# A delta-rule attention kernel: one product of K with [Q | state] in four 64x64 places, with a new order of program blocks

## The chip, the cores and the metric

The kernel runs on one core of a Trainium2 chip. The metric is the device time of one execution in microseconds (us). A kernel is timed in several runs; the median is compared. One further execution is profiled, and all views of the trace come from it.

The engines have short names: PE is TensorE (matrix products), PEld its weight load, DVE is VectorE, ACT is ScalarE, POOL is GpSimd, SP is SyncE, which here only starts DMA transfers.

## The reference

Two parts follow each other. The first is linear attention with the delta rule: 4 batches x 8 heads, 768 tokens, head width 48, float32.

```python
for t in range(S):
    y[:, :, t] = q_t @ state                       # per head, state is 48x48
    v_old = k_t @ state                            # k normalized
    state = state + b_t * outer(k_t, v_t - v_old)
```

The second part takes y (4 x 768 x 384) through a mixture of four softmax attentions ("experts" of width 64), each with its own projections, causal over all 768 tokens, with the top two of four gates per token, and an output projection:

```python
for e in range(4):
    q, k, v = x @ wq[e], x @ wk[e], x @ wv[e]
    a = softmax(causal(q @ k.T / 8))
    out += gate[..., e] * (a @ v @ wo[e])
```

## The kernel before

**The delta rule in chunks.** The tokens of a head are cut into chunks of 64. Within a chunk the recurrence is a triangular system; so a chunk needs K Kᵀ (64x64), its inverse T, a masked K Qᵀ, and the state that the chunk before left. The 32 heads are in two groups of 16; a *unit* n (0 to 5) is one group and 256 tokens, so units 0, 1, 2 follow each other in one group and 3, 4, 5 in the other. A unit has four chunks c (0 to 3). A chunk handles 16 heads at once: eight pairs p, and in each pair f = 0 or 1, of which one lies on partitions 0 to 63 and the other on 64 to 127. A head of 48 features uses 48 of its 64 rows.

**The steps of a unit, by their names in the code** (n is the unit, c the chunk):

- `ga`: K Kᵀ on PE; `ge`, `ad`, `ae`, `al` copy it out of PSUM.
- `bi`, `nm`, `sv`, `bo`, `tn`: norms and a triangular solve of all 512 blocks of 32x32 of the unit at once, each block in a lane of 32x32 numbers in the buffer `b`. Steps `sv.n.1` to `sv.n.30` are an elimination on POOL, two instructions each; `bi` transposes into the lane buffer on DVE, `bo` and `tn` out of it. There is one lane buffer for units 1 to 5. Unit 0 is solved by another, shorter way (`s0` on DVE, `p1`, `p2`, `p3` on PE).
- `m1`, `we`, `m2`, `me`: the off-diagonal blocks of T (PE, ACT).
- `vs`: v is scaled by the norm (POOL).
- `gp`: K Qᵀ on PE, and `pm`: times the causal mask, written over Q in the tile `qp` (DVE). Neither needs the state.

Then the chain through the chunks, which does: `ks` (K times state, PE), `xs` (v minus that, DVE), `tx` (times T, PE), `us` (copy, DVE and ACT), `ku` (into the state, PE, added up in PSUM bank 0), `se` (the new state out of PSUM, ACT), and from there the next chunk's `ks`. `yy` (PE) makes the outputs y, `yh`, `yl`, `hx` split them into a high and a low part and lay them out for the second part.

**The second part** has the steps `pj` (projections to q and k), `pv` (v and gate logits), `mx`, `mz`, `mr` (a row maximum), `sc` (scores), `ex` (exp), `av` (times V), `ft`, `fo` (output projection), `so` (store), and some small ones; `pj`, `pv`, `mx`, `sc` and `fo` use a product that takes one pass, the others on PE float32 in two passes.

**Places of the array.** A product with at most 64 rows and 64 weight columns uses a 64x64 quarter of PE's array: rows 0 to 63 or 64 to 127, by the partitions of its operands, and columns 0 to 63 or 64 to 127, by the partitions of its result. `feat(f)` are the 48 feature rows of side f, `tok(f)` the 64 token rows on the *other* side. So `gp`, `ks`, `ga` and `ku` each use two places, from one side to the other, in turn:

```python
for p in range(NP):
    for f in range(2):
        mm(g[tok(f), p], k[feat(f), p], z[feat(f), f, p])      # ks
```

**Order.** The whole program is one list of words, `ORDER`. A word is a step with its numbers, and after an @ the PSUM banks that it uses (`ks.1.2@5`). The steps are issued in this order, and each engine runs its own in this order. `fl.k` issues k products of zeros of 128x128 on PE, whose result nobody reads.

Of the kernel before, what the change touches and what calls it, by code (L numbers as in the profile page):

```python
# [12 lines left out]
OP = mybir.AluOpType  # L13
# [8 lines left out]
RK, RQ, RV, RA, RG = 5, 6, 3, 3, 3  # L22
# [5 lines left out]
zz.6 lk.0.0 zb sq0 lk.0.1 zz.2 lk.0.2 zz.0 lk.0.3 le.1.2 zz.5 le.1.1 le.1.3 zz.4 le.1.0 fl.47@2 ga.0.0@1 lc.2 ga.0.1@2  # L28
ae.0.2 lc.1 ae.0.0 le.2.2 ga.0.2@3 ae.0.1 lq.0.0 ae.1.1 ae.1.2 ga.0.3@4 ae.1.0 ae.2.3 lv.0.0 ae.2.0 le.2.1 ae.2.1
ga.1.2@5 ae.3.3 ae.2.2 lq.0.2 ae.1.3 ae.3.1 ga.1.1@6 ae.0.3 ae.3.0 lq.0.3 ae.3.2 al.3.3 ga.1.3@7 bi.0 al.3.1 lk.1.0  # L30
ge.1.2 ga.1.0@4 lq.1.0 ad.1.3.2 ad.1.2.1 nm.0.0 ge.1.3 nm.0.1 ad.1.3.0 ad.1.3.3 nm.0.2 ci ga.2.2@7 ge.1.0 zz.1 ww.1
lq.0.1 nm.0.3 ad.1.0.2 ad.1.2.3 bs ad.1.0.0 ad.1.2.0 gp.0.0@4 ad.1.3.1 le.2.0 ad.1.2.2 lt.0.1 al.1.1 s0.1 ad.1.0.3
ga.2.1@5 le.2.3 al.1.3 s0.2 ge.1.1 ww.0 ad.1.0.1 s0.3 gp.0.2@2 lk.1.1 ad.1.1.2 s0.4 ad.1.1.1 al.2.3 s0.5 ad.1.1.0
ad.1.1.3 al.0.1 s0.6 gp.0.3@6 ge.2.2 a2 s0.7 al.0.3 bi.1 al.2.1 vs.0.0 wh.1 ge.2.1 wl.1 gp.0.1@7 s0.8 nm.1.0 s0.9
gp.1.0@1 zz.7 ww.3 nm.1.1 lq.1.1 ga.2.0@5 nm.1.2 lv.0.1 ga.2.3@3 sv.1.0 lc.0 lv.0.2 wh.0 lt.0.0 s0.10 sv.1.1 ge.2.0
s0.11 sv.1.2 s0.12 sv.1.3 s0.13 s0.14 sv.1.4 s0.15 gp.1.1@5 sv.1.5 bo.0 ax sv.1.6 ge.2.3 wh.3 wl.0 tn.0 p1.2@3 w1.2
vs.0.1 ww.2 lt.0.2 p1.0@3 sv.1.7 pm.0.0.0 w1.0 pm.0.0.1 p2.0@3 sv.1.8 pm.0.1.1 p3.0@4 sv.1.9 w2.0 w3.0.1 m1.0.0@3
w3.0.0 sv.1.10 we.0.0 tc0.0.1 m2.0.0@3 tc0.0.0 p1.1@4 sv.1.11 me.0.0.1 me.0.0.0 tx.0.0@3 w1.1 wl.3 p2.1@4 us.0.0.0
us.0.0.1 le.3.0 sv.1.12 wh.2 pm.0.3.1 sv.1.13 p3.1@3 w2.1 ku.0.0 tc0.1.1 w3.1.0 vs.0.2 tc0.1.0 w3.1.1 m1.0.1@4
# [846 lines left out]
```

## Time and profile before

| what | value |
|---|---|
| median of 3 runs | 448.96 us (446.31 to 453.4) |
| the profiled execution | 453.23 us |
| its span, first to last instruction | 451.2 us |
| PE, DVE, POOL, ACT busy | 421.4, 283.8, 218.1, 202.1 us |
| mean granted clock of PE | 0.936 |
| DMA | 65853 packets, 40.02 MB |

The profile lists instructions in groups: line, engine, operation, result <- operands, the shapes, the count. Every product in the source appears in the trace as two where it is float32. Nearly all PE instructions stand on line 187, which is the helper `mm`, so PE's groups are told apart by the tiles' names: `z,kf` is `ks`, `qp,kf` is `gp`, `x,gf` is `tx`, `z,kv` is `ku`, `qp,z` is `yy`, `gf` alone is `ga`, `zb` is a filler. The granted clock is 1.00 when PE runs at its full clock.

### The profile page before, as it was taken

Reading aid. Unit: us, or ns where it says so; the run is one execution under the profiler, and the core shown is the slowest. Engines: PE = TensorE matmul, PEld = TensorE weight load, DVE = VectorE, ACT = ScalarE, POOL = GpSimd, SP = SyncE. Lnnn points to the kernel's source line nnn. Section 1 sums busy time; section 2 is a strip of 40 time slices with the busy share of each in tenths; the row PEclk is TensorE's granted clock in tenths of the full one; section 3 lists DMA queues with packets and bytes.
Section 4 is the critical chain, followed back from the end, with each engine's and each line's share of the span. In section 5 each row is a group of like instructions: output and inputs, shape, how many; then the busy total and the mean of one; then the engine's idle time right before and its main releaser. Section 6 shows DMA issues by size and latency. Waiting matters only on the chain.

```text
span 451.2 us, 21660 instructions
## 1 busy us (share of the span) xinstructions
PE 421.4 (93%) x9677; PEld 380.7 (84%) x9677; DVE 283.8 (63%) x566; ACT 202.1 (45%) x415; POOL 218.1 (48%) x417
## 2 busy tenths in 40 slices
PE   8756998979999999999799999999999999999997
PEld 8745997979999878988778899899988889978996
DVE  2894355574777896369568799267671467448621
ACT  3832253465435336544434445254552434533552
POOL 4559783258884288752588521798630100201010
PEclk9895558699999999999999999999996999999999
DMA  7861135433643424217550241623171310000101
GB/s 209 230 191 46 38 96 136 116 101 83 156 122 85 86 90 86 68 53 185 150 166 4 76 83 31 136 58 109 40 173 36 101 36 3 21 0 36 38 3 72
DMA packets 65853, 40.02 MB, mean 89 GB/s; under 512 B 45536, under 2 KB 57696, under 8 KB 65760
## 3 DMA queue, kind: packets, MB, share of 16 engines
q1 hardware_dynamic: 65760, 38.63, 32.4%
q8 instruction: 76, 1.25, 1.2%
q14 instruction: 17, 0.14, 0.1%
HBM read 26.29 MB, written 4.72 MB: 69 GB/s over the span
## 4 chain that ended last, share of the span: by engine, by line
PE 78%; DMA 4%; SPq 4%; DVE 4%; issue 3%; POOL 3%; ACT 2%; DVEq 0%; ACTq 0%; POOLq 0%
PE p L187 76%; DMA gf<-in_kq_dram 1%; SPq L625 1%; POOL tm L497 1%; POOL b L499 1%; DMA xu<-h 1%; DVE z L583 1%; SPq L267 1%; ACT z L189 1%; PE p L802 1%; DMA qp<-in_kq_dram 1%; SPq L488 1%; PE p L727 1%; DMA kf<-in_kq_dram 1%; POOL wl L302 1%
## 5 line engine op out<-in xcount | busy, mean ns | idle before, releaser
L497 POOL TENSOR_TENSOR tm<-b 128x30 f32<-128x30 f32 (+9 forms) x150 | 72.8, 485 | 35.5 <-DVE b L493 25.4
L499 POOL TENSOR_TENSOR b<-b,tm 128x30 f32<-128x30 f32 (+9 forms) x150 | 77.5, 517 | 11.8
L763 ACT ACTIVATE at<-p 128x768 f32<-128x768 f32 (+1 forms) x48 | 43.0, 916 | 31.3 <-DVE p L768 15.9
L189 ACT ACTIVATE z<-p 48x384 f32<-48x384 f32 (+1 forms) x68 | 32.9, 484 | 48.0 <-PE p L187 38.0
L718 DVE TENSOR_REDUCE mp<-p 128x2 f32<-128x1024 f32 (+3 forms) x40 | 44.6, 1116 | 3.2 <-PE p L187 2.4
L187 PE MATMUL p<-vs,at 128*64 128x65 f32 x1344 | 44.8, 223 | 0.6 <-DVE h L617 0.6
L187 PEld LDWEIGHTS p<-vs,at 128*64 128x64 f32 x1344 | 41.4, 137 | 3.5 <-issue 1.2
L187 PE MATMUL p<-xu,wh 128*128 128x512 f32 (+1 forms) x168 | 41.4, 389 | 1.4 <-issue 1.4
L187 PEld LDWEIGHTS p<-xu,wh 128*128 128x128 f32 x168 | 30.0, 206 | 7.6 <-DMA xu<-h 1.6
L360 DVE TENSOR_TENSOR qp<-p,cs 64x512 f32<-64x512 f32 x48 | 32.1, 684 | 5.9 <-PE p L187 5.4
L561 POOL TENSOR_TENSOR kv<-kv,nt 128x384 f32<-128x384 f32 x24 | 19.8, 831 | 33.1 <-DMA kv<-in_kv_dram 24.9
L187 PE MATMUL p<-qp,kf 48*64 48x64 f32 x768 | 28.7, 224 | 4.0 <-DMA qp<-in_kq_dram 3.3
L187 PEld LDWEIGHTS p<-qp,kf 48*64 48x64 f32 x768 | 25.7, 138 | 5.4 <-issue 3.4
L570 DVE TENSOR_TENSOR x<-kv,p 128x384 f32<-128x384 f32 x22 | 12.1, 550 | 26.8 <-PE p L187 18.2
L187 PE MATMUL p<-qh,kh 64*128 64x128 f32 (+1 forms) x192 | 28.8, 297 | 0.0
L187 PE MATMUL p<-z,kf 48*64 48x48 f32 x704 | 26.7, 228 | 1.9 <-issue 1.9
L187 PE MATMUL p<-qp,z 128*48 128x64 f32 (+1 forms) x768 | 28.4, 232 | 0.1
L768 DVE TENSOR_TENSOR p<-p,km 128x512 f32<-128x512 f32 x24 | 16.7, 697 | 18.2 <-PE p L187 17.9
L187 PEld LDWEIGHTS p<-z,kf 48*64 48x64 f32 x704 | 24.2, 144 | 4.2 <-issue 3.1
L583 DVE COPY z<-p 64x384 f32<-64x384 f32 x24 | 13.5, 560 | 22.4 <-PE p L187 11.0
L187 PE MATMUL p<-wh,xu 128*128 128x260 f32 x144 | 27.0, 300 | 0.2 <-DMA xu<-h 0.2
L187 PE MATMUL p<-qh,kl 64*128 64x128 f32 (+1 forms) x192 | 26.8, 276 | 0.0
(159 smaller groups left out, 976.8 us busy)
## 6 DMA issues: line engine op xcount, KB each, us to landing
kv<-in_kv_dram SPq DMA_DIRECT2D x46, 192.0 KB, 3.3
kf<-in_kq_dram SPq DMA_DIRECT2D x24, 224.0 KB, 3.2
out_dram<-ot SPq DMA_DIRECT2D x24, 192.0 KB, 2.0
gf<-in_kq_dram SPq DMA_DIRECT2D x20, 224.0 KB, 3.7
qp<-in_kq_dram SPq DMA_DIRECT2D x36, 96.0 KB, 2.6
xu<-h SPq DMA_DIRECT2D x72, 32.0 KB, 2.5
da<-gf SPq DMA_DIRECT2D x16, 128.0 KB, 3.6
gf<-dg SPq DMA_DIRECT2D x16, 128.0 KB, 3.8
```

Source lines behind the costliest of these rows:

```text
L187: T.matmul(o, lhsT=a, rhs=b, start=start, stop=True, skip_group_check=True)
L189: copy = lambda o, a: S.activation(o, a, AF.Copy)
L267: nc.sync.dma_start(QP[zi(n, c) % RQ][64 * f:64 * f + w, f], kq[n, c, 64 * f:64 * f + w, 512:1024].rearrange("p (a b) -> p a b", a=NP))
L360: V.tensor_tensor(QP[zi(n, c) % RQ][r, f], slots(("gp", n, c), NP, 64)[r], PMK[r, None, :].to_broadcast([64, NP, 64]), op=OP.mult)
L497: G.tensor_tensor(tv, B2[:, i:i + 1, i + 1:].to_broadcast([128, i, m]), B2[:, 0:i, i:i + 1].to_broadcast([128, i, m]), op=OP.mult)
L499: G.tensor_tensor(B2[:, 0:i, i + 1:], B2[:, 0:i, i + 1:], tv, op=OP.add)
L561: G.tensor_tensor(vt, vt, NRM[n % 2][:, c * NP:c * NP + NP, None].to_broadcast([128, NP, HD]), op=OP.mult)
L570: V.tensor_tensor(X, KV[zi(n, c) % RV][:, 1], slots(("ks", n, c), NP, HD), op=OP.subtract)
L583: V.tensor_copy(o, a)
L718: V.tensor_reduce(o[:, :, y0:y0 + per], g, axis=AXL.X, op=OP.max, negate=True)
L763: S.activation(at(n, b, y, kp)[:, :, 0:w], P8[:, b0:b0 + 2, 0:w], AF.Exp, scale=0.125)
L768: V.tensor_tensor(g, g, KM[:, None, None, :].to_broadcast([128, 2, 2, 128]), op=OP.add)
```

## The change

`gp` and `ks` become one step `gk`: K is the weight once, and the moving operand is [Q | state], 64 + 48 = 112 columns. To this end the state moves from its own tile `z` into the tile `qp`, behind Q. In the same step half of the pairs (p < 4) keep their results on their own side of the partitions, the other half goes across as before, so that four places are used in turn instead of two; the results of the two halves lie in two PSUM banks. `tx` and the copies follow these places, `pm` has four pieces per chunk instead of two, and K Kᵀ (`ga`) is made per two chunks and half of the pairs. The lane buffer is doubled: odd and even units have one each. `qp` has 4 buffers instead of 6, `kf` 4 instead of 5. The first clears of the state are done by DVE instead of POOL.

```diff
-RK, RQ, RV, RA, RG = 5, 6, 3, 3, 3
+RK, RQ, RV, RA, RG = 4, 4, 3, 3, 3
...
+def gr(f, p):
+    return slice(64 * f, 64 * f + 64) if p < 4 else tok(f)
...
-    QP = [sb(f"qp{i}", 2, NP, 64) for i in range(RQ)]
+    QP = [sb(f"qp{i}", 2, NP, 112) for i in range(RQ)]
-    B = sb("b", 1024)
+    B = [sb(f"b{i}", 1024) for i in range(2)]
-    Z = [sb(f"z{i}", 2, NP, HD) for i in range(2)]
...
+    def zs(i):
+        return QP[i % RQ][:, :, :, 64:112]
...
-    def gp(n, c):
-        g, k, q = slots(("gp", n, c), NP, 64), KF[zi(n, c) % RK], QP[zi(n, c) % RQ]
-        for p in range(NP):
-            for f in range(2):
-                mm(g[tok(f), p], k[feat(f), p], q[feat(f), f, p])
+    def gk(n, c):
+        b, a, q = BK["gk", n, c][0], KF[zi(n, c) % RK], QP[zi(n, c) % RQ]
+        w = 64 if first(n, c) else 112
+        for i in range(4):
+            for x in range(2):
+                p = 4 * x + i
+                for f in range(2):
+                    mm(P8[gr(f, p), b + x, 112 * i:112 * i + w], a[feat(f), p], q[feat(f), f, p, 0:w])
...
-    def ks(n, c):
-        g, k, z = slots(("ks", n, c), NP, HD), KF[zi(n, c) % RK], Z[zi(n, c) % 2]
-        for p in range(NP):
-            for f in range(2):
-                mm(g[tok(f), p], k[feat(f), p], z[feat(f), f, p])
...
     def tx(n, c):
-        g, x = slots(("tx", n, c), NP, HD), KV[zi(n, c) % RV][:, 1] if first(n, c) else X
-        for p in range(NP):
-            for f in range(2):
-                mm(g[tok(f), p], GF[n % RG][tok(f), NP * c + p], x[tok(f), p])
+        b, v = BK["tx", n, c][0], KV[zi(n, c) % RV][:, 1] if first(n, c) else X
+        for i in range(4):
+            for x in range(2):
+                p = 4 * x + i
+                for f in range(2):
+                    r = gr(f, p)
+                    mm(P8[tok(f), b + x, 48 * i:48 * i + 48], GF[n % RG][r, NP * c + p], v[r, p])
```

The list `ORDER` is written anew. What moves is seen best in the order of instructions on two engines. (The numbers behind the names count tiles: `kf_64` to `kf_68` are the K tiles, `gf` hold K Kᵀ and T, `qp` Q, `p_63` is PSUM, `vs` and `at` in the start hold unit 0's blocks. A count x16 is 16 products in the source.)

PE in the start, from K Kᵀ of unit 1 (`gf_79`) to the solve of unit 0, before:

```order
L187 MATMUL p_63<-gf_79 64x64 x64
L187 MATMUL p_63<-gf_80 64x64 x16
L187 MATMUL p_63<-qp_69,kf_64 64x64 x16
L187 MATMUL p_63<-gf_80 64x64 x16
L187 MATMUL p_63<-qp_71,kf_66 64x64 x16
L187 MATMUL p_63<-qp_72,kf_67 64x64 x16
L187 MATMUL p_63<-qp_70,kf_65 64x64 x16
L187 MATMUL p_63<-qp_73,kf_68 64x64 x16
L187 MATMUL p_63<-gf_80 64x64 x32
L187 MATMUL p_63<-qp_74,kf_64 64x64 x16
L187 MATMUL p_63<-gf_78,vs 32x32 x64
```

And PE at the same place now: the K Kᵀ products of unit 2 (`gf_77`), then 179 fillers on the zero tile `zb`, of which the first rows are shown; the products of unit 0's solve stand behind them.

```order
L198 LDWEIGHTS zb
L198 MATMUL p_63<-zb 128x128
L198 MATMUL p_63<-gf_77 64x64 x64
L198 LDWEIGHTS zb
L198 MATMUL p_63<-zb 128x128
L198 LDWEIGHTS zb
L198 MATMUL p_63<-zb 128x128
```

Six `gp` stood here, of unit 0 and of the first half of unit 1; now no product with Q does, since `gk` needs the state.

PE in chunk 2 of unit 1, before: `ku` and `yy` of chunk 1 (`z_100,kv_77`, `qp_74,z_100`), `gp` of a chunk of unit 2, `ks` of this chunk (`z_99,kf_65`), `ga` of a later unit, and `tx` (`x,gf_79`).

```order
L187 MATMUL p_63<-z_100,kv_77 48x48 x16
L187 MATMUL p_63<-qp_74,z_100 48x64 x16
L187 MATMUL p_63<-qp_73,kf_64 64x64 x16
L187 MATMUL p_63<-z_99,kf_65 64x48 x16
L187 MATMUL p_63<-gf_79 64x64 x16
L727 MATMUL p_63<-cs,mp_121 128x128 x2
L187 MATMUL p_63<-x,gf_79 64x48 x16
```

And PE in the same chunk now: `ku` and `yy` of chunk 1, then `gk` of this chunk, `ga` of a later unit, `tx`.

```order
L198 MATMUL p_63<-qp_69,kv_74 48x48 x16
L198 MATMUL p_63<-qp_69 48x64 x16
L198 MATMUL p_63<-qp_70,kf_66 64x112 x16
L198 MATMUL p_63<-gf_76 64x64 x16
L198 MATMUL p_63<-x,gf_76 64x48 x16
L198 MATMUL p_63<-kh,qh 128x128 x4
L198 MATMUL p_63<-wh_132,xu_97 128x260 x3
```

The product with Q has moved from any earlier place into the chain of the states, and is one with the product with the state.

DVE in the same chunk, before (`pm` writes `qp`, `xs` writes `x`, `us` writes `z`):

```order
L360 TENSOR_TENSOR qp_73<-p_63,cs 64x512
L570 TENSOR_TENSOR x<-kv_75,p_63 128x384
L619 TENSOR_TENSOR xu_102<-p_63,xu_102 112x2x3x64
L617 TENSOR_TENSOR h_103<-p_63,h_103 112x2x64
L360 TENSOR_TENSOR qp_73<-p_63,cs 64x512
L661 COPY lg_126<-p_63 128x4
L583 COPY z_99<-p_63 64x384
```

And DVE in chunks 0 and 1 of unit 0 now: the four pieces of `pm` ahead of `us`, whose result is now in `qp`, and in chunk 1 between `xs` and `us`.

```order
L391 TENSOR_TENSOR qp_68<-p_63,cs 64x4x64 x4
L615 COPY qp_68<-p_63 64x8x48
L489 TENSOR_TENSOR gf_75<-gf_75,p_63 128x8x32
L493 TENSOR_TENSOR tn<-tn,p_63 32x256 x2
L595 TENSOR_TENSOR x<-kv_73,p_63 128x384
L391 TENSOR_TENSOR qp_69<-p_63,cs 64x4x64 x4
L489 TENSOR_TENSOR gf_75<-gf_75,p_63 128x8x32
L615 COPY qp_69<-p_63 64x8x48
```

The mask step belongs to the chunk at hand now, not to a later one, and stands in the way of its `us`.

More of the change, by code (lines that the diff above doesn't have):

```diff
@@ L306, in zb @@
         V.memset(ZB, 0.0)
+        V.memset(P8[:, 7], 0.0)
     def ex0():
@@ L315, in zz @@
         if k < 2:
-            G.memset(Z[k], 0.0)
+            for i in (k, k + 2):
+                V.memset(zs(i), 0.0)
         elif k == 2:
@@ L358, in pm, with ga @@
-    def pm(n, c, f):
-        r = tok(f)
-        V.tensor_tensor(QP[zi(n, c) % RQ][r, f], slots(("gp", n, c), NP, 64)[r],
-                        PMK[r, None, :].to_broadcast([64, NP, 64]), op=OP.mult)
-    def ae(c, q):
-        r, t = slice(32 * q, 32 * q + 32), slice(NP * c, NP * c + NP)
-        o, a = AD[r, t], slots(("ga", 0, c), NP, 64)[r, :, 32 * (q % 2):32 * (q % 2) + 32]
+    def ga(n, k, x):
+        g = slots(("ga", n, k, x), NP, 64)
+        for j in range(2):
+            c = 2 * k + j
+            a = GF[n % RG][:, NP * c:NP * c + NP] if n else KF[zi(n, c) % RK]
+            for i in range(4):
+                p = 4 * x + i
+                for f in range(2):
+                    mm(g[gr(f, p), 4 * j + i], a[feat(f), p], a[feat(f), p])
@@ new lines, in gs, with half, ge @@
+    def gs(n, k, x):
+        return slots(("ga", n, k, x), NP, 64).rearrange("p (c i) j -> p c i j", c=2)
+    def half(a, k, x):
+        return a.rearrange("p (c x i) j -> p c x i j", x=2, i=4)[:, 2 * k:2 * k + 2, x]
+    def ge(n, k, x):
+        copy(half(GF[n % RG], k, x), gs(n, k, x))
+    def gk(n, c):
[6 more added lines that the diff above has]
+                    mm(P8[gr(f, p), b + x, 112 * i:112 * i + w], a[feat(f), p], q[feat(f), f, p, 0:w])
@@ new lines, in gv, with pm, ae @@
+    def gv(n, c):
+        b = BK["gk", n, c][0]
+        return P8[:, b:b + 2, 0:448].rearrange("p x (i d) -> p x i d", d=112)
+    def pm(n, c, f, x):
+        r = gr(f, 4 * x)
+        V.tensor_tensor(QP[zi(n, c) % RQ][tok(f), f, 4 * x:4 * x + 4, 0:64], gv(n, c)[r, x, :, 0:64],
+                        PMK[r, None, :].to_broadcast([64, 4, 64]), op=OP.mult)
+    def ae(k, x, q):
+        r = slice(32 * q, 32 * q + 32)
+        o, a = half(AD, k, x)[r], gs(0, k, x)[r, :, :, 32 * (q % 2):32 * (q % 2) + 32]
@@ L367, in ae @@
         if q % 2:
+            copy(o, a)
+        else:
             V.tensor_copy(o, a)
-        else:
-            copy(o, a)
     def ax():
@@ L378, in a2, with al @@
                         op=OP.mult)
-    def al(c, q):
+    def al(k, x, q):
         r = slice(32 * q, 32 * q + 32)
-        copy(AL[c][r], slots(("ga", 0, c), NP, 64)[r, :, 0:32])
+        copy(AL[2 * k + x][r], slots(("ga", 0, k, x), NP, 64)[r, :, 0:32])
     def root(g0, r, ss):
@@ L472, in gd, with ad @@
             nc.sync.dma_start(DA[r], GF[n % RG][r, :, o:o + 32])
-    def ad(n, c, q):
-        r, t, o = slice(32 * q, 32 * q + 32), slice(NP * c, NP * c + NP), 32 * (q % 2)
+    def ad(n, k, x, q):
+        r, o = slice(32 * q, 32 * q + 32), 32 * (q % 2)
         if q % 2:
-            G.tensor_copy(DA[r, t], GF[n % RG][r, t, o:o + 32])
+            G.tensor_copy(half(DA, k, x)[r], half(GF[n % RG], k, x)[r, :, :, o:o + 32])
         else:
-            copy(DA[r, t], slots(("ga", n, c), NP, 64)[r, :, o:o + 32])
+            copy(half(DA, k, x)[r], gs(n, k, x)[r, :, :, o:o + 32])
     def tc(n, k, q):
@@ L842, in _layout @@
     feat_ = lambda x: x.transpose(0, 4, 5, 3, 8, 1, 2, 6, 7).reshape(NU, CH, 2, HD, 1, NP * 64)
-    tok_ = lambda x: x[:, :, :, ::-1].transpose(0, 4, 5, 3, 6, 7, 1, 2, 8).reshape(NU, CH, 128, 1, NP * HD)
+    tok_ = lambda x: x.transpose(0, 4, 5, 3, 6, 7, 1, 2, 8).reshape(NU, CH, 128, 1, NP * HD)
+    cross = lambda x: x[:, :, :, ::-1]
+    side = lambda x: np.concatenate([x[:, :1], cross(x[:, 1:])], 1)
     kq = np.zeros((NU, CH, 2, 64, 2 * NP * 64), np.float32)
@@ L846, in _layout @@
     a = {"kq": kq.reshape(NU, CH, 128, -1),
-         "kv": np.concatenate([tok_(k), tok_(v)], 3).reshape(NU, CH, 128, -1)}
-    a["beta"] = b[:, :, :, ::-1].transpose(3, 6, 5, 1, 2, 0, 4, 7, 8).reshape(128, NU * 32)
+         "kv": np.concatenate([tok_(cross(k)), tok_(side(v))], 3).reshape(NU, CH, 128, -1)}
+    a["beta"] = side(b).transpose(3, 6, 5, 1, 2, 0, 4, 7, 8).reshape(128, NU * 32)
     rows = []
```

324 lines of the change are left out of this document (165 added, 159 removed).

## The prediction

> **What bounds the kernel now.** I read the page first: busy shares and the clock row.
>
> ```profile
> span 451.2 us, 21660 instructions
> PE 421.4 (93%) x9677; PEld 380.7 (84%) x9677; DVE 283.8 (63%) x566; ACT 202.1 (45%) x415; POOL 218.1 (48%) x417
> PEclk9895558699999999999999999999996999999999
> ```
>
> TensorE (PE) is busy 93% of the span, no other engine above 63%. The clock row has a hole in slices 4 to 8, so next I cut the span into stages with the view that sums an engine by windows (columns: window, its length, PE busy, granted clock, DMA share, GB/s).
>
> ```profile
> 45.10:63.00 17.90, 17.24 (x462) 0.50 0.18 54
> 63.00:76.00 13.00, 11.56 (x444) 0.89 0.40 115
> 76.00:90.00 14.00, 13.91 (x226) 0.63 0.59 134
> 90.00:103.60 13.60, 11.11 (x406) 0.87 0.34 98
> 103.60:451.00 347.40, 335.68 (x7187) 0.99 0.30 77
> ...
> 32.00:34.00 2.00, 0.00 (x0) 0.50 0.00 0
> 64.00:66.00 2.00, 2.00 (x104) 0.51 0.40 110
> 66.00:68.00 2.00, 2.00 (x70) 1.00 0.05 13
> 74.00:76.00 2.00, 0.70 (x26) 1.00 0.79 248
> 76.00:78.00 2.00, 1.91 (x29) 0.55 1.13 218
> ```
>
> The timeline of PE (start, duration, group, wait) gives the borders: the first product that needs unit 0's solve, the first `tx` of unit 0, a wait that I come back to, and the first `tx` of unit 1.
>
> ```profile
> 34.34 1.08 PE L187 MATMUL p<-gf,vs 32*32 32x32 f32 x64 [3.32 <-DVE gf L432]
> 45.10 1.95 PE L187 MATMUL p<-kv,gf 64*64 64x48 f32 x32 [0.17 <-POOL tm L497]
> 76.09 1.32 PE L187 MATMUL p<-xu,wh 128*128 128x256 f32 x5 [1.39 <-issue]
> 103.64 0.96 PE L187 MATMUL p<-x,gf 64*64 64x48 f32 x26
> ```
>
> So there are three stages. Until 45.1 the solve of unit 0 and the start of the lane chain of unit 1 set the pace. From 45.1 to 103.6 PE is busy, but at half clock for much of it: the clock drops to 0.50 with the wait of 3.32 us that ends at 34.3 and comes back only at 66; it drops again behind the wait of 1.39 us at 76. From 103.6 to the end, 347.4 us, PE is busy 335.7 at a clock of 0.99: there the time is PE's work, and nothing else.
>
> **The price of a PE step.** The timeline of PE, one contiguous stretch at full clock. A step is 16 products in the source; each float32 product is two passes, so x32. A step costs the distance from its start to the next start.
>
> ```profile
> 118.71 0.92 PE L187 MATMUL p<-z,kv 64*48 64x48 f32 x32
> 119.56 1.10 PE L187 MATMUL p<-qp,z 128*48 128x64 f32 x32
> 120.59 1.15 PE L187 MATMUL p<-qp,kf 48*64 48x64 f32 x32
> 121.57 1.09 PE L187 MATMUL p<-z,kf 48*64 48x48 f32 x32
> 122.49 1.11 PE L187 MATMUL p<-gf 48*64 48x64 f32 x32
> ...
> 123.90 1.14 PE L187 MATMUL p<-x,gf 64*64 64x48 f32 x32
> 124.97 0.33 PE L187 MATMUL p<-qh,kh 64*128 64x128 f32 x2
> ```
>
> `ku` 0.85, `yy` 1.03, `gp` 0.98, `ks` 0.92, `tx` 1.07 us. Each of these uses two places of the array, so 16 passes per place: 61 ns per pass in `gp`, 53 in `ku`, 64 in `yy`.
>
> **The change part by part.** (1) `gk` in the place of `gp` and `ks`: 16 products of 112 columns in four places, 8 passes per place. From `ku` (48 columns) to `yy` (64 columns, equal weights of 48) a pass grows by 11 ns, 0.7 ns per column. An estimate for 112 columns is 61 + 48 x 0.7 = 94 ns, times 8 = 0.75, plus 0.1 for the change of shape: **0.85 us**. (2) `tx` in four places: 8 x 67 ns = **0.54** instead of 1.07. Both hold if four places run side by side. Two rows bear on it. First, small tiles: 64 passes in four 32x32 places, then 32 passes in two.
>
> ```profile
> 73.13 0.75 PE L187 MATMUL p<-at,tn 32*32 32x32 f32 x64
> 73.70 0.68 PE L187 MATMUL p<-tn,at 32*32 32x32 f32 x32
> 74.31 0.38 PE L187 MATMUL p<-xu,wh 128*128 128x256 f32 x1
> ```
>
> 64 passes took 0.57, 32 took 0.61: doubling the places halved the pass. But those four places share neither rows nor columns; in `gk` every place shares its rows with one and its columns with another. Sharing rows is what `yy` does (two column places below all 128 rows): 1.03, as much as `gp`, whose places share nothing. Sharing columns is what the scores do, in two banks:
>
> ```profile
> 250.26 0.28 PE L187 MATMUL p<-qh,kh 64*128 64x256 f32 x2
> 250.38 0.28 PE L187 MATMUL p<-ql,kh 64*128 64x256 f32 x2
> ...
> 239.13 0.52 PE L187 MATMUL p<-wl,xu 128*128 128x260 f32 x3
> 239.48 0.52 PE L187 MATMUL p<-wh,xu 128*128 128x260 f32 x3
> ```
>
> A pair of 256 columns each starts 0.12 us after the last pair; products of 260 columns that use the whole array start 0.35 / 3 = 0.12 apart. So each kind of sharing is free alone; both at once no row shows. Bounds for `gk`: 0.55 if width is free (`ks` against `gp`: 48 against 64 columns, 0.92 against 0.98), 3.0 if the four take turns (32 x 94 ns). I take 0.85, nearest to the rows of two places.
>
> The Trainium skill, "TensorE: Matmul & The Clock Gate", Part 3, speaks against this change: a weight load overlaps matmuls in flight only when their row group differs. By that rule `yy`, whose passes all use every row, could overlap nothing: 48 weight and 64 moving columns in turn, at 61 ns per 128, would make 32 x 53 ns = 1.7 us. It took 1.03, so this trace speaks against the rule here. What it would make of the sum is the second rival.
>
> (3) The order. Up to the first `tx` of unit 1 the two orders hold the same PE steps, except: 8 `gp` and 4 `ks` before, 5 `gk` now, and 386 small filler products on zeros instead of 50. After it: 16 `gp` and 18 `ks` become 19 `gk`, 20 `tx` change their price, and there are 101 fillers instead of 47. A filler at full clock:
>
> ```profile
> 443.93 1.73 PE L187 MATMUL p<-zb 128*128 128x128 bf16 x28
> 445.47 0.60 PE L187 MATMUL p<-wh,oh 128*128 128x384 f32 x2
> ```
>
> 1.54 / 28 = 55 ns. **Sum behind 103.6:** 16 x 0.98 = 15.7 and 18 x 0.92 = 16.6 go, 19 x 0.85 = 16.2 comes, 20 x 0.53 = 10.6 goes, 54 x 0.055 = 3.0 comes: **-23.7 us**, all of it on the path, since PE is the bound there.
>
> (4) Ahead of 45.1, six `gp` ran early while PE had nothing else to do; their removal gains nothing, and a block of 179 fillers (9.8 us) stands there instead, ahead of the first products that need unit 0's solve (34.3 before). Unit 0's first scaling of v is now queued on POOL behind 14 of the 31 elimination steps of unit 1, which puts the first `tx` at about 46, as before. If that cover is gone it is a loss of as much as it is late.
>
> (5) From 45.1 to 103.6 the full-clock work of PE is busy times clock: 17.24 x 0.50 + 11.56 x 0.89 + 13.91 x 0.63 + 11.11 x 0.87 = 37.3 us in 58.5. The steps of this stage change by -2 `gp` (2.0; six of the eight lie earlier), -4 `ks` (3.7), +4 `gk` (3.4; one lies earlier), -4 x 0.53 (2.1), +49 fillers (2.7): 35.6. At full clock without a gap the first `tx` of unit 1 would start at 46 + 36 = 82. The other floor is the lane chain: it ends on POOL at 72 and is taken up on DVE at 80.1, late.
>
> ```profile
> 70.73 1.26 POOL L501 TENSOR_SCALAR_AFFINE_SELECT b<-b 128x1024 f32<-128x1024 f32 x1
> 80.14 1.22 DVE L503 TENSOR_TENSOR b<-b,aa 128x1024 f32<-128x1024 f32 x1
> ```
>
> Behind it come the scaling, two transposes of 2 us and the products of unit 1's solve, some 10 us: 82 again. With a clock held most of the time I take 90.6: **-13 us** (bounds 0, if the clock falls as before, and -20). The skill's same page, Part 1, says that about 3.4 us of sustained matmuls lift the clock; here 17.9 us, 96% of them busy, did not, so I do not count on it once the clock is down.
>
> (6) DVE: the mask step becomes 96 pieces of half the size instead of 48.
>
> ```profile
> L360 DVE TENSOR_TENSOR qp<-p,cs 64x512 f32<-64x512 f32 x48 | 32.1, 684 | 5.9 <-PE p L187 5.4
> L713 DVE TENSOR_TENSOR p<-p,qm 128x256 f32<-128x256 f32 x16 | 6.8, 428 | 3.6 <-PE p L187 3.5
> ```
>
> 96 x 0.428 = 41.1 against 32.8 (48 x 0.684): +8.3 us on an engine that was busy 284 of 451; it lies beside PE's work. But all four pieces (1.7 us) stand at many places between the subtraction that feeds `tx` and the copy that drains it, where `tx` alone needs 0.54. I add **+4** for gaps, a third of the 11.7 us that PE was idle behind 103.6 (bounds 0 and 22, third rival). Queries now land beside the state in rows of 112, in pieces of 256 bytes instead of 2 KB; the 24 loads move as many bytes and are issued some steps ahead: 0. The four clears of the state move from POOL to DVE ahead of the first data: 0. The second lane buffer lets unit 3's transpose stand inside unit 2's chain; PE is the bound there: 0.
>
> Sum against the profiled execution, 453.2 (span 451.2 plus 2.0): 453.2 - 13 - 23.7 + 4 = **420.5**. That execution was 0.94% above the median of the three, 448.96; scaled by it, **417 us**.
>
> **The rivals.** First, *the clock falls all the same* and the middle stage keeps its 58.5 us: 433.5, scaled 429. For it: the drop at 76 came after a wait of only 1.39 us. Against: the fillers stand at those waits.
>
> Second, *a row group serves one place at a time*, weight load and products in turn. Then 61 ns is 64 + 64 columns, and 64 + 112 is 84 ns, 16 per row group: `gk` 1.44, `tx` 1.07. Behind 103.6: -32.3 + 27.4 + 3 = -1.9; the middle stage gains 13 - 4 x 0.59 - 2.1 = 8.5, and 4 for gaps: 447, scaled 443: no change. This is the skill's rule from Part 3; for it speaks that no row shows four such places, against it `yy`. It is also the case in which the change does not do what it says.
>
> Third, *the chain through DVE becomes the bound*: 1.1 us later per chunk (1.7 - 0.54), 20 chunks, 22 us instead of 4: 438.5, scaled 434. Against: PE has other work queued at nearly all of these places.
>
> Fourth, the other side: *the four places take turns* altogether, `gk` 3.0. Behind 103.6: -32.3 + 57 + 3 = +27.7, the middle stage gains nothing: 481, scaled 476. With `tx` unchanged, the whole change stops paying from a `gk` of 1.7 us, and is 2% slower from 2.1.
>
> **How the numbers follow.** Forecast 0.50, clock 0.15, row group 0.13, DVE chain 0.12, turns 0.10. 2% (440 to 458) is what a measurement here can tell from no change. Faster: 0.49 + 0.14 + 0.03 + 0.09 = 0.75; slower 0.11; same 0.14. Range: low with `gk` 0.55 and the middle stage at its floor, 453.2 - 20 - 29.4 + 2 = 406, scaled 402; high at the second rival, 443. Above it lies the fourth, 0.10, and a little of the others.
>
> **What would show it.** In the profile after: a group of 112 columns, x704, about 0.85 from start to start; 64x48 products of `x,gf` at 0.54; granted clock near 1 from 34 to 100 us; the first `tx` of unit 1 at about 90; behind it some 328 us. I am wrong if `gk` is above 1.2, if the block of fillers runs at half clock and ends behind 36 us, or if PE is below 94% busy behind the first `tx` of unit 1.

## The result, and the profile after

The changed kernel takes **434.3 us** (median of 4 runs, 429.0 to 435.1), the kernel before 448.8 in the same rounds: a ratio of 0.967, 95% interval 0.957 to 0.977. Two further sets, in five rounds each, gave 0.9645 (0.961 to 0.969) and 0.9695 (0.964 to 0.975). It is faster by some 15 us. The forecast was 417, a gain of 32: the time lies inside the range (402 to 443), but less than half of the gain came. Some executions of either kernel are slower, at a lower granted clock; the ratios leave these out, the medians do not.

The page of the changed kernel (profiled execution 435.13 us), the lines that answer to those of before:

```profile
span 433.4 us, 21046 instructions
PE 402.7 (93%) x9363; PEld 355.8 (82%) x9363; DVE 297.5 (69%) x619; ACT 203.5 (47%) x415; POOL 219.4 (51%) x415
PEclk9899699989999999999899999999999999999999
```

PE is as busy as before, 93%, but with 19 us less; DVE has 14 us more; the hole in the clock row is gone but for slice 5.

Next the view by windows, cut at the first `tx` of unit 0 and of unit 1 (window, length, PE, PEld, DVE, ACT and POOL busy, granted clock, DMA share, GB/s). First the kernel before, then the changed one:

```profile
0.00:45.10 45.10, 31.88 (x976) 30.17 (x976) 28.01 (x67) 21.02 (x49) 27.72 (x57) 0.81 0.61 169
45.10:103.64 58.54, 53.86 (x1530) 49.83 (x1530) 33.19 (x64) 26.41 (x59) 32.77 (x58) 0.71 0.36 97
103.64:451.20 347.56, 335.63 (x7183) 300.68 (x7173) 222.64 (x435) 154.66 (x308) 157.62 (x304) 0.99 0.30 77
```

```profile
0.00:50.44 50.44, 42.93 (x1102) 40.82 (x1102) 31.09 (x73) 22.89 (x52) 30.22 (x61) 0.90 0.59 142
50.44:98.50 48.06, 41.33 (x1516) 37.19 (x1515) 30.67 (x66) 25.74 (x58) 28.59 (x49) 0.96 0.36 99
98.50:433.40 334.90, 318.45 (x6751) 277.79 (x6747) 235.73 (x481) 154.83 (x305) 160.64 (x307) 0.99 0.34 83
```

The start is 5.3 us longer, the middle stage 10.5 shorter, the rest 12.7 shorter. In the last stage PE's busy time fell by 17.2 us, and 4.5 of them became time in which PE is not busy.

The prices, on the timeline of PE (start, duration, group), and the groups of `gk` and of the mask step:

```profile
66.42 1.00 PE L198 MATMUL p<-qp,kf 48*64 48x112 f32 x32
67.34 0.90 PE L198 MATMUL p<-zb 128*128 128x128 bf16 x13
...
47.71 2.80 PE L198 MATMUL p<-zb 128*128 128x128 bf16 x28
50.44 0.68 PE L198 MATMUL p<-kv,gf 64*64 64x48 f32 x32
51.05 0.75 PE L198 MATMUL p<-at,tn 32*32 32x32 f32 x64
```

```profile
L198 PE MATMUL p<-qp,kf 48*64 48x112 f32 x704 | 22.9, 262 | 0.5
L391 DVE TENSOR_TENSOR qp<-p,cs 64x256 f32<-64x256 f32 x96 | 40.4, 421 | 12.0 <-PE p L198 10.3
```

`gk` takes 0.92 us from its start to the next start, `tx` 0.61. The mask step costs 40.4 us in 96 pieces of 0.421; 41.1 were forecast. The block of 28 fillers ahead of the first `tx` of unit 0 takes 2.73 us, 1.8 times the 1.54 us of such a block at full clock: the granted clock over it is 0.58.

The view of waits of PE's weight loads behind the first `tx` of unit 1 (releaser: us, times, longest), the largest of before and then of the changed kernel:

```profile
PEld p L187 <- issue: 13.4, 40, 1.9
PEld p L187 <- DVE z L583: 2.9, 6, 0.6
PEld p L187 <- ACT z L189: 1.0, 2, 0.7
```

```profile
PEld p L198 <- issue: 12.8, 46, 0.8
PEld p L198 <- DVE qp L615: 3.5, 8, 0.8
PEld p L198 <- ACT ot L200: 3.2, 2, 3.0
PEld p L198 <- DVE lg L693: 2.0, 3, 1.5
PEld p L198 <- ACT qp L200: 1.7, 6, 0.4
```

Over all releasers the sum is 23.3 us before and 32.2 now; waits for DVE rose from 6.4 to 10.4, for ACT from 2.0 to 8.7. No single one is large.

### The profile page after: what moved, and what is told of

It is laid out like the page before. It is cut to its first block, busy times and chain, and to the rows that moved or that the text cites. A ratio compares the mean times of both kernels' runs of the same rounds, so it can differ in the third digit from the quotient of the medians.

```text
span 433.4 us, 21046 instructions
## 1 busy us (share of the span) xinstructions
PE 402.7 (93%) x9363; PEld 355.8 (82%) x9363; DVE 297.5 (69%) x619; ACT 203.5 (47%) x415; POOL 219.4 (51%) x415
## 4 chain that ended last, share of the span: by engine, by line
PE 57%; DVE 11%; POOL 8%; issue 4%; DMA 2%; ACT 2%; SPq 1%; DVEq 0%; ACTq 0%; POOLq 0%
PE p L198 55%; POOL b L530 4%; POOL tm L528 3%; DVE qp L391 2%; DVE dg L463 1%; DVE qp L615 1%; DMA out_dram<-ot 1%; PE p L834 1%; ACT qp L200 1%; SPq L657 1%; DVE tn L466 1%; DVE x L595 1%; DVE mq L750 1%; DMA gf<-dg 1%; DMA xu<-h 1%
## 5 line engine op out<-in xcount | busy, mean ns | idle before, releaser
L200 ACT ACTIVATE qp<-p 48x384 f32<-48x384 f32 (+1 forms) x68 | 32.9, 483 | 43.9 <-PE p L198 32.3
L391 DVE TENSOR_TENSOR qp<-p,cs 64x256 f32<-64x256 f32 x96 | 40.4, 421 | 12.0 <-PE p L198 10.3
L198 PE MATMUL p<-xu,wh 128*128 128x512 f32 (+1 forms) x168 | 39.5, 373 | 0.0
L198 PE MATMUL p<-zb 128*128 128x128 bf16 x487 | 34.3, 232 | 2.5 <-issue 1.4
L198 PEld LDWEIGHTS <-zb 128*128 128x128 bf16 x487 | 30.7, 105 | 3.8 <-issue 1.7
L198 PE MATMUL p<-qp 128*48 128x64 f32 (+1 forms) x768 | 27.7, 224 | 0.8 <-issue 0.5
L198 PE MATMUL p<-ql,kh 64*128 64x128 f32 (+1 forms) x192 | 27.4, 275 | 0.0
L198 PE MATMUL p<-mr,sl 64*128 64x128 f32 (+1 forms) x192 | 27.3, 274 | 0.0
L198 PEld LDWEIGHTS p<-qp 128*48 128x48 f32 (+1 forms) x768 | 24.3, 126 | 2.8 <-issue 1.1
L198 PE MATMUL p<-qp,kv 64*48 64x48 f32 x704 | 21.9, 209 | 4.9 <-DVE qp L615 2.9
```

The source lines that it names most:

```text
L198: T.matmul(o, lhsT=a, rhs=b, start=start, stop=True, skip_group_check=True)
L200: copy = lambda o, a: S.activation(o, a, AF.Copy)
L391: V.tensor_tensor(QP[zi(n, c) % RQ][tok(f), f, 4 * x:4 * x + 4, 0:64], gv(n, c)[r, x, :, 0:64], PMK[r, None, :].to_broadcast([64, 4, 64]), ...
```

## The experiments

Two theories stood at the start. *PE theory*: the forecast's, PE's work is the time behind the first `tx` of unit 1, and what is missing was lost in the start and to fillers. *Chain theory*: waits for other engines set the pace there, and PE's work is only partly on the path. Times are medians; a ratio is to the kernel before in the same rounds. "Behind" is the time from the first `tx` of unit 1 to the end, from the profiled execution; it is 347.6 before. It is one execution each time: the three profiles of the changed kernel that were taken give 334.9, 334.5 and 336.6, so a difference of 2 us there says little. "PE's idle time" is the sum of the waits of PE that the view of waits lists, and "by PE's rows" sums each product from its start to the next start, without idle time.

### The changed kernel again

> The changed kernel once more, in more rounds, as the yardstick for the runs beside it. If the small gain was the luck of four runs, the ratio to before comes out near 0.93 (what was forecast); if it is real, 0.965 to 0.97 again, 434 us.

432.3 us, ratio 0.9645: the smaller gain is real. In its profile "behind" is 334.5, against 334.9 in the first one. These are the yardsticks of the runs below.

### Two places instead of four

```diff
     def gk(n, c):
...
-        for i in range(4):
-            for x in range(2):
+        for x in range(2):
+            for i in range(4):
                 p = 4 * x + i
```

(The same swap in `tx`.)

> gk and tx take their pairs in an order in which only two places of the array alternate (all pairs of one half first); the same products, banks and order of steps otherwise. If the four places are what made gk and tx cheap, gk goes from 0.93 us (start to next start) to about 1.5 (16 passes of 94 ns) and tx from 0.61 to 1.07. PE theory (PE's work is the bound behind the first tx of unit 1): 19 x 0.57 + 20 x 0.46 = 20 us more there and some 4 more in the middle stage, 455 to 458 us. Chain theory (waits for DVE and ACT set the pace now, and PE has slack): under half of it, 440 to 446 us. If the places do nothing, no change in either price.

437.8 us, ratio 0.977 (0.972 to 0.982): 5.5 us more than the changed kernel in the same rounds. On its timeline of PE:

```profile
113.56 0.95 PE L198 MATMUL p<-x,gf 64*64 64x48 f32 x32
114.44 0.44 PE L198 MATMUL p<-kh,qh 64*128 64x128 f32 x4
...
118.51 1.43 PE L198 MATMUL p<-qp,kf 48*64 48x112 f32 x32
119.87 0.63 PE L198 MATMUL p<-wh,xu 128*128 128x260 f32 x3
```

`gk` costs 1.36 and `tx` 0.88. So the order with four places is faster by a factor of 1.44 to 1.48, not 2. (It also writes two PSUM banks in turn where this run writes half a step into each, so that places and banks change together; no run parts the two.) The Trainium skill, "TensorE: Matmul & The Clock Gate", Part 3, says that a weight load overlaps matmuls in flight only when the row group differs; the second rival was built on it and came to 1.44 and 1.07 for four places. The trace disagrees with that: 0.92 and 0.61, where every row group serves two places. With one place for each row group, as in this run, that rival's price does hold: 1.36 us for 16 passes is 85 ns a pass, and it had 84.

Behind the first `tx` of unit 1 the two steps together take 11.7 us more by PE's rows, but the stage grows by 4.2, a little over a third; PE's idle time there falls from 11.2 to 6.8. This is the chain theory's outcome, and more of it than expected: the time lies below the 440 to 446 us put down for it.

### The mask step narrowed, and moved

```diff
-        V.tensor_tensor(QP[zi(n, c) % RQ][tok(f), f, 4 * x:4 * x + 4, 0:64], gv(n, c)[r, x, :, 0:64],
+        w = 64 if n == 0 else 1
+        V.tensor_tensor(QP[zi(n, c) % RQ][tok(f), f, 4 * x:4 * x + 4, 0:w], gv(n, c)[r, x, :, 0:w],
```

> Left out: from unit 1 on the mask step pm treats one column of 64 instead of all, so K Q is neither masked nor copied there and y is not the reference's. pm's 80 pieces fall from 0.42 us to 0.1 or less, some 26 to 30 us of DVE work, most of it between xs and us. Chain theory (the four pieces ahead of us cost the missing time behind the first tx of unit 1, where the idle time and the other steps came out 9 us above the forecast): 6 to 12 us less than the changed kernel, 423 to 428 us. PE theory (the pieces lie beside PE's work): within 3 us of the changed kernel.

430.6 us, 1.7 less than the changed kernel; "behind" 331.3, 3.2 less. DVE's work fell by 20 us, not by 26 to 30. It misses the 6 to 12 us of the chain theory as I had put it: the mask step is not the chain.

The order alone, in 11 chunks (`pm` behind `us`):

```diff
-xs.1.3 pm.1.3.1.1 mo.0.0 fl.8@3 tx.1.3@67 lg.0.1.1 ve.0.1.1 pm.1.3.0.1 sv.2.23 pm.1.3.1.0 sc.0.0.0.0@23 pm.1.3.0.0 le.4.3 us.1.3.1 us.1.3.0
+xs.1.3 mo.0.0 fl.8@3 tx.1.3@67 lg.0.1.1 ve.0.1.1 sv.2.23 sc.0.0.0.0@23 le.4.3 us.1.3.1 us.1.3.0 pm.1.3.1.1 pm.1.3.0.1 pm.1.3.1.0 pm.1.3.0.0
```

> Order only: in 11 of the 24 chunks the pieces of pm that stood ahead of us on DVE are issued behind it (where no later step takes the PSUM banks of gk first). Chain theory through DVE: us comes 0.4 to 1.7 us earlier in these chunks, 37 pieces x 0.42 = 15.5 us less ahead of us, and a third of it comes through: 3 to 5 us less, 427 to 429 us. If DVE's place in the chain costs nothing: 432, as the changed kernel.

435.9 us, ratio 0.977 (0.972 to 0.981): slower than the changed kernel, a miss. PE now waits for `pm` itself, for `yy`, which needs the masked rows, and once for 1.8 us ahead of a score product that takes the PSUM banks of `gk` next:

```profile
PE p L198 <- issue: 7.9, 7, 3.4
PE p L198 <- DVE qp L391: 4.2, 8, 1.8
PE p L198 <- DVE qp L615: 2.1, 6, 0.5
```

### The fillers

Without the 101 behind the first `tx` of unit 1 (words like `fl.18@5` struck out):

> Without the 101 fillers behind the first tx of unit 1. PE theory: they are work on the path at 55 ns each, 101 x 0.055 = 5.5 us less, 429 us. Cover theory: they stand in waits that are there anyway, no change (434). Clock theory: without them the granted clock falls at the waits, as it did at 76 us in the kernel before, and the time is longer by 5 us or more.

433.9 us, ratio 0.968: nothing. By PE's rows 6.6 us went, and PE's idle time behind rose from 11.2 to 15.8. The mean clock there stayed at 0.99. I had charged the 54 of these fillers that are new with 3 us of path; they stand in waits.

Without the 326 in the start and the middle stage:

> Without the 326 fillers between the first block of 60 and the first tx of unit 1. Clock theory (they hold the granted clock up, and this is where the 10 us of the start and middle stage come from): the clock falls to 0.50 at the wait for unit 0's solve (about 25 to 36 us) and stays there for some 30 us as in the kernel before; the first tx of unit 1 comes 8 to 12 us later, 441 to 445 us. Rival (28 of them at half clock stand right ahead of the first tx of unit 0, and they cost as much as they hold): first tx of unit 0 at 46 to 47 instead of 50, first tx of unit 1 within 2 us of where it was, 431 to 434 us.

429.6 us, ratio 0.965 (0.958 to 0.972): the same as with them, inside the interval. The clock did what its theory says, the time did not:

```profile
48.00:52.00 4.00, 3.82 (x156) 3.50 (x153) 0.98 (x2) 1.42 (x3) 3.69 (x6) 0.50 0.15 40
52.00:56.00 4.00, 4.00 (x154) 3.66 (x148) 2.31 (x6) 2.21 (x7) 3.76 (x6) 0.50 0.20 47
...
28.00:63.00 35.00, 22.51 (x847) 20.81 (x849) 16.91 (x40) 11.91 (x28) 31.63 (x55) 0.52 0.44 109
47.18:94.03 46.85, 41.18 (x1462) 37.22 (x1463) 30.56 (x66) 25.95 (x59) 30.87 (x52) 0.84 0.36 101
```

From 28 to 63 us the clock is 0.52, and over the middle stage 0.84 instead of 0.96; yet the first `tx` of unit 0 comes at 47.2 and that of unit 1 at 94.0, both earlier than with the fillers. In the changed order this stage does not hang on the clock.

With 44 instead of 60 ahead of the first K Kᵀ, and without the 11 and 28 ahead of the first `tx`:

> A candidate for a faster version, the full computation: 44 instead of 60 fillers ahead of the first K K products (the first block ended at 6.67 and the products followed it with no wait), and without the 11 and 28 fillers ahead of the first tx of unit 0 (2.8 us at half clock). If the start's chain passes into the end: first tx of unit 0 at 46 to 48, 2 to 4 us less than the changed kernel, 428 to 430 us. If what follows absorbs it: 432.

433.0 us, ratio 0.976 (0.971 to 0.981): no gain, though the start came out as expected. The first `tx` of unit 0 and that of unit 1:

```profile
46.22 1.10 PE L198 MATMUL p<-kv,gf 64*64 64x48 f32 x32
...
93.56 0.68 PE L198 MATMUL p<-x,gf 64*64 64x48 f32 x32
```

Some 4 us earlier at both places, and given back behind (338.2 against 334.5). The fillers thus explain why the start was late, and the start does not explain the end.

**Fillers in the kernel before**, the other way round:

```diff
-s0.11 sv.1.2 s0.12 sv.1.3 s0.13 s0.14 sv.1.4 s0.15 gp.1.1@5 sv.1.5 bo.0 ...
+s0.11 sv.1.2 s0.12 sv.1.3 s0.13 s0.14 sv.1.4 s0.15 fl.80@5 gp.1.1@5 sv.1.5 bo.0 ...
...
+fl.26@0 p1.2@3 ... fl.20@0 p2.0@3 ... fl.12@0 m1.0.0@3 ... fl.21@0 m2.0.0@3 ... fl.10@0 tx.0.0@3
```

> The kernel before with 169 more fillers at the waits around the solve of unit 0 (80 ahead of the last early gp, 26 ahead of the first product of the solve, 63 between there and the first tx of unit 0), the rest of the order as it was. Clock theory (the half clock from 34 to 66 us makes the middle stage long): with the clock near 1 that stage falls from 58.5 to 48 us or so, 8 to 10 us less than before, ratio 0.98. Rival (the chain of waits in the order of before sets it): the stage stays within 3 us of 58.5, ratio 0.995 to 1.005.

443.6 us, ratio 0.982 (0.972 to 0.993): 6 us by the medians, 8 by the ratio, as the clock theory said.

```profile
0.00:46.67 46.67, 41.00 (x1144) 39.37 (x1144) 28.10 (x67) 21.23 (x49) 29.14 (x58) 0.89 0.61 163
46.67:96.31 49.64, 46.19 (x1531) 42.65 (x1529) 32.31 (x63) 25.89 (x58) 28.51 (x48) 0.86 0.41 110
```

The middle stage falls from 58.5 to 49.6 us. So fillers alone get back 6 to 8 us of the kernel before (by the interval of the ratio 3 to 13), with the clock of that stage at 0.86 instead of 0.71. The changed order gets as much with or without fillers: PE is busy there for 41.2 us in the run without them, against 53.9 and 46.2. Whether the merged step or the new order does that, no run separates; the four places do not (47.7 us with two).

### The lane chain and the second lane buffer

```diff
-            m = 31 - i
+            m = min(31 - i, 2) if n > 1 else 31 - i
```

> Left out: from unit 2 on, each elimination step on POOL treats at most 2 of up to 30 columns, so T and y are not the reference's. POOL's chain of a unit shrinks from about 36 us to some 20. Lane chain theory (behind the first tx of unit 1, PE now waits for the next unit's solve at the units' borders, which took the place of the PE work removed): the time falls by 8 us or more, to 424 or below, and the stretches from the first tx of unit 1 to that of unit 2, and from that of unit 3 to that of unit 4, shrink. PE theory: no change within 2 us.

429.9 us, ratio 0.964: 2.4 us less by the medians, nothing by the ratio, and "behind" 334.3, as in the changed kernel. POOL's work fell from 219.4 to 159.8 us:

```profile
PE 398.9 (93%) x9363; PEld 351.9 (82%) x9363; DVE 296.9 (69%) x619; ACT 203.4 (47%) x415; POOL 159.8 (37%) x415
```

POOL's chain sets nothing behind the first `tx` of unit 1.

One lane buffer (`B = [sb("b", 1024)] * 2`, and `bi.3` behind `tn.2`):

> One lane buffer for units 1 to 5 instead of two: unit 3's transpose into it stands behind unit 2's last transpose out of it, everything else in the same order. My forecast put the second buffer at nothing: 432 us. If unit 3's chain is what the middle of the program waits for: the first tx of unit 3 comes 2 to 5 us later, and the time is longer by as much.

434.7 us, ratio 0.970 (0.962 to 0.979): no difference from the changed kernel that this run can tell, as forecast. "Behind" is 338.7, so a loss of a few us is not excluded.

### Three reliefs at once

> Three of the earlier edits at once: pm on one column from unit 1 on, the short elimination from unit 2 on, and no fillers behind the first tx of unit 1 (left out: the mask step and most of the elimination, so y and T are not the reference's). Alone they gave -1.7, -2 and +1.6 us against the changed kernel. If one chain binds: the sum of the three, -2 to -4 us, 428 to 430. If several chains lie behind each other, so that relief of one only shows the next: -8 us or more, 424 or below.

430.3 us, ratio 0.967 (0.960 to 0.975): no more than each alone. Nothing larger hides behind these three.

### PE's work taken away beside the chain

```diff
     def pj(n, m, h, q):
         w = 512 if h == 2 else 256
         g = bank(("pj", n, m, h), w)
+        if q == 2:
+            return
...
     def pv(n, hb, b):
         g, x = bank(("pv", n, hb, b), 260), XU[n % 2]
-        for q in range(3):
+        for q in range(2):
```

In the kernel before:

> The kernel before, with a third of the work of pj and pv left out (of the three products of high and low parts the one with a low part that stands last; y is less exact). Behind the first tx of unit 1 this removes (48.2 + 26.7) / 3 = 25.0 us of PE's work, as much as the change was to remove there (23.7), but none of it on the chain through the chunks. My step in the prediction (behind 103.6 the time is PE's work and nothing else): 25 us less there, ratio to before 0.93 to 0.945, 416 to 423 us. Rival (PE's 97% busy hides chains that lie just behind it, and only a third comes through, as with two places): 8 to 10 us less, ratio 0.975 to 0.985.

432.5 us, ratio 0.974 (0.968 to 0.980): 11.6 us less by the ratio, 9 to 14 by its interval. By PE's rows `pj` and `pv` took 21.3 us less behind the first `tx` of unit 1 (74.9 to 53.6) and 3.6 less ahead of it, so 24.9 were left out and about half came back, 0.36 to 0.57. The one profile, of the slowest of the four executions (437.35 us), gives more for that stage alone:

```profile
103.35:435.40 332.05, 316.93 (x7042) 282.42 (x7035) 223.53 (x435) 154.16 (x308) 158.86 (x304) 0.98 0.31 80
```

That is 15.5 us less than the 347.56 before, 0.7 of the 21.3. Ahead of it nothing came back (103.35 for 103.64), with the clock of the middle stage at 0.65 instead of 0.71. This tests my step in the kernel that I read it from, and it fails there: not all of PE's work was on the path, but a half to seven tenths, while PE was 97% busy. The rival's third was too low.

In the changed kernel:

> The same third of pj and pv left out of the changed kernel: (48.5 + 26.9) / 3 = 25.1 us of PE's work behind the first tx of unit 1. PE theory: 405 to 410 us. If the waits already bind in the changed kernel (two places: 12.7 us of added PE work cost 5.5): 10 us or less, 422 to 428 us, and PE's waits grow by 15 us.

427.8 us, ratio 0.960 (0.953 to 0.968); "behind" 327.4, 7.1 less than 334.5. Both kernels were then run side by side on one chip:

> The changed kernel, on the chip and in the rounds of the run beside it: ratio to before 0.965, 432 to 435 us.

> The changed kernel without a third of pj and pv (24 us of PE's work: 21.5 behind the first tx of unit 1, 2.8 ahead of it). If the waits set the pace, as the runs so far say: 4 to 8 us less than the run beside it. PE theory: 20 us or more.

435.9 and 426.9 us, ratios 0.9695 (0.964 to 0.975) and 0.951 (0.947 to 0.956): 8 to 9 us. "Behind" of the two, in this order:

```profile
98.19:434.80 336.61, 321.11 (x6747) 280.49 (x6747) 236.29 (x481) 155.08 (x305) 160.90 (x307) 0.98 0.33 83
96.23:423.10 326.87, 300.56 (x6609) 259.71 (x6609) 236.25 (x480) 154.81 (x305) 160.02 (x307) 0.98 0.34 85
```

By PE's rows `pj` and `pv` took 20.4 us less there (13.4 + 7.0); the stage lost 9.7, and PE's idle time rose from 10.7 to 21.7. With the 3.3 us that went ahead of the stage, 8 to 9 of 23.7 us came through, a little over a third, as in the run with two places. For the stage alone it is a third to a half (7.1 of 21.7 in the run above, 9.7 of 20.4 here), against 0.7 in the one profile of the kernel before; by the whole times the intervals do not tell the two kernels apart.

### DVE's work taken away

```diff
-        V.tensor_reduce(o[:, :, y0:y0 + per], g, axis=AXL.X, op=OP.max, negate=True)
+        V.tensor_reduce(o[:, :, y0:y0 + per], g[:, :, :, 0:16], axis=AXL.X, op=OP.max, negate=True)
```

(and the mask step on one column, as above).

> Left out in the changed kernel: pm on one column from unit 1 on, and the row maximum mr over 16 of the keys instead of up to 512 (y and the scale of the exponentials are not the reference's). DVE's work falls by 20 + 30 us or so, from 298 to about 248. DVE theory (DVE's own order of work sets the pace behind the first tx of unit 1): 12 to 20 us less than the changed kernel, 412 to 420 us. If DVE is not it: 428 to 431, as with pm alone.

> The same relief of DVE, and the third of pj and pv left out as well (25 us of PE's work). If PE and DVE each hide behind the other: more than the sum of the two alone, 20 us or more less than the changed kernel, 412 or below. If the latency of the chain through the chunks in a fixed order sets the pace: about the sum of both alone (5 for the PE work and what the run beside it gives), 422 to 426.

> The kernel before with the same relief of DVE (pm on one column from the seventh chunk on, mr on 16 keys): some 45 us of DVE's work less. PE theory for the kernel before: ratio 0.99 to 1.0. If DVE took part in the pace already: 0.97 to 0.98.

430.8 us (ratio 0.957, 0.948 to 0.966), 420.8 (0.934, 0.926 to 0.942), and for the kernel before 446.4 (0.996, 0.992 to 1.001). The "behind" stages, in this order:

```profile
97.31:428.30 330.99, 317.91 (x6747) 279.23 (x6747) 176.14 (x480) 155.26 (x305) 160.44 (x307) 0.98 0.34 84
95.21:414.50 319.29, 297.88 (x6621) 259.59 (x6618) 175.94 (x480) 154.96 (x305) 160.56 (x308) 0.99 0.35 87
101.16:445.20 344.04, 332.91 (x7180) 298.79 (x7173) 165.63 (x435) 154.70 (x308) 155.35 (x300) 1.00 0.30 78
```

DVE lost 60 of 236 us there, and the stage 3.5. Alone DVE is not the bound; the "DVE theory" of 12 to 20 us is out. With PE's work taken away as well the stage lost another 11.7. Against 334.5, the two alone take 3.5 and 7.1 to 9.7, both together 15.2: a little more than the sum, far from the 20 and more that would show two engines hidden behind each other. The kernel before is 3.5 us shorter in that stage with the same relief, but its ratio shows no clear change. What binds the rest is neither engine's total; it fits the latency of steps issued in a fixed order, each waiting for one of several engines, but no run takes that latency away by itself, so it stays open.

## Why the prediction was wrong, step by step

- **Prices: nearly right, in part by luck.** `gk` 0.92 for 0.85, `tx` 0.61 for 0.54. I had put a pass of 112 columns at 94 ns and four places at twice the pace of two; the pass costs 85 ns, and four places bring a factor of 1.44 to 1.48. For `gk` the two errors offset each other in part. By PE's rows the changed steps behind the first `tx` of unit 1 came to 17.6 (`gk`) - 16.7 (`gp`) - 19.3 (`ks`) - 6.9 (`tx`) = -25.3 us, with the added fillers -21.8, where -23.7 was forecast.
- **"All of it on the path, since PE is the bound there": this step failed.** That stage fell by 12.7 us (13.1 in the second profile), not by 23.7 less 4. Of the 7.0 us that are missing there, 1.9 are prices; the other 5.1 are the term "+4 for gaps", which came to 9.1 (from -21.8 to -12.7). Of these 9.1, 4.5 are time in which PE is not busy and 4.6 a stretching of steps that did not change; PE's weight loads wait 8.9 us longer. I had read 335.7 us busy of 347.4 as "PE's work and nothing else". A run that takes PE's work away tests such a reading, and in the kernel before it returned a half to seven tenths; 12.7 of 21.8 is 0.58. None of my signs of being wrong showed this: `gk` stayed below 1.2, the block of 179 fillers ran at a clock of 1.00 and ended at 34.8, and PE is still 95% busy behind the first `tx` of unit 1 (318.45 of 334.90). The Trainium skill, "Perfetto Trace Analysis", section "Identifying the Most-Contended Engine", warns that the busy share of matmuls is no good measure of how close a kernel is to the roofline, and has one use MFU (the FLOPs done against the peak) and the busy share of weight loads instead. That share is 84% before and 82% after here, against 93% and 93% for the matmuls. The runs agree with the warning, but neither share gives the part that came back.
- **"+4 for gaps", the third rival.** The rival's direction was right, the engine wrong: DVE's own work is worth 2 to 4 us, as I had charged, and not the 22 of a DVE chain. That its 434 us is the time measured is chance. The remaining loss is spread over many short waits.
- **Middle stage: the size nearly right, the reason wrong.** Forecast 58.5 to 44.6 (from 46 to 90.6), measured 48.1 and 47.3. The clock was indeed what made it long before (fillers alone: 49.6), but the changed kernel does not need it (46.9 with the clock at 0.84 over the stage, and at half in its first 15 us).
- **Start: 4 us late.** Forecast 46, measured 50.4. I costed the fillers at nothing: K Kᵀ followed the first block with no wait, and most of the last 28 ran at half clock right ahead of the first `tx`, after PE had idled at 40 us. With 16 fewer in the first block and without the last 11 and 28 it is 46.2, but the end does not move; no run separates the three.
- **Scaling.** I divided by the 0.94% by which the profiled execution of before lay above its median. The profiled execution after lay 0.2% above its own, so this took 3.5 us off the forecast for nothing.

Together: 8 us in the start and middle stage, 7 behind and 3.5 by scaling, less the 1 us by which the profiled execution lies above the median, make up the 17 us between 417 and 434.

## What to carry to other kernels

A busy share near 100% says that an engine is never long without work, not that its work is the time: where many steps are issued in a fixed order, take away work of that engine beside the chain, and see how much comes back, before pricing a change at one to one. Here it was a half to seven tenths in the kernel before and a third to a half in the changed one. And fillers that hold the clock were worth 6 to 8 us in one order of steps and nothing in the other, so they too are to be tried, not assumed.

## What the runs showed that I had not expected

- `tx` in two places costs 0.88 us when its results lie in two banks, half a step in each, and 1.07 in the kernel before, where all lie in one; no run tells whether the banks or the places do it.
- The granted clock fell to 0.50 in the changed kernel at about 43 us, behind 2 us in which PE was busy for 0.37 (40 to 42), and was back at 1.00 by 50 us; without the fillers it stayed at 0.50 for more than 30 us with PE busy 64% of that time.
- Idle time of PE that no semaphore explains ("issue") is 10.8 us in 12 pieces, as much as before (11.7), most of it ahead of the first `tx` of unit 1. No run tried it.
